# SwiGLU feed-forward on one core: the first rows of x by plain loads and TensorE transposes instead of transposing loads

**Chip, cores, metric.** One core of a Trainium2 chip (trn2). The metric is the device time of one execution in microseconds (us). One core has no neighbour to compare with here, so an execution is called slow only when it lies over 1.5% above the fastest of the same kernel. The kernel before spreads over some 2% by itself (127.79 to 130.0 in 16 executions), so for it the rule cuts the top of an even spread rather than a separate state.

## The reference

```python
B, S, D, F = 1, 2048, 512, 1376          # bf16
def reference(x, w_gate, w_up, w_down):
    g = silu(x @ w_gate)
    u = x @ w_up
    return (g * u) @ w_down
```

## The kernel before

S is cut into 4 blocks of 512 rows, F into 11 tiles of 128 (the last has 96). A unit is one F tile of one block: 4 gate matmuls and 4 up matmuls over the 4 columns of 128 of D (c0 to c3), then silu on ScalarE and the product on VectorE. After 11 units, four row tiles go through the down matmuls. The matmuls need x transposed, which the load does.

```python
N_WARM = 7
xt_pieces = [(0, 0, NDC // 2), (0, NDC // 2, NDC)] + [(cs, 0, NDC) for cs in range(1, NCS)]

def xt_piece(eng, i):                       # transposing load
    cs, c0, c1 = xt_pieces[i]
    eng.dma_start_transpose(
        out=xT_sb[:, cs, c0:c1, :],
        in_=x2d[cs * NT : (cs + 1) * NT, c0 * P : c1 * P],
    ).then_inc(xt_sems[i], 16)

# SyncE's queue
xt_piece(sp, 0)
xt_piece(sp, 1)
for i in range(2, len(w_pieces)):
    w_piece(sp, "g", i)
    w_piece(sp, "u", i)
wd_load(sp)
for i in range(2, len(xt_pieces)):
    xt_piece(sp, i)
# ... cut: the stores of the output

# ScalarE's queue: the first weights
w_piece(act, "g", 0); w_piece(act, "u", 0); w_piece(act, "g", 1); w_piece(act, "u", 1)

# TensorE
def stage1(u):
    cs, fi = divmod(u, NFC)
    pi = piece_of(fi * P)
    wait_w("wg", pi)
    for c in range(NDC):
        wait_xt(cs, c)
        mm1(u, c, "g", (act_done, u - 1) if (c == 0 and u >= 2) else None)
    wait_w("wu", pi)
    for c in range(NDC):
        mm1(u, c, "u", (dve_done, u - 1) if (c == 0 and u >= 2) else None)

for i in range(N_WARM):
    pe.matmul(ps_w[:, 0, :], lhsT=ones_w, rhs=ones_m, start=True, stop=True)
# ... cut: 4 blocks of 11 x stage1 and 4 x stage2
```

## Time and profile before

| | before |
|---|---|
| time, 16 executions | 127.79 to 130.0, median 129.04 |
| the four known at the prediction | 127.96, 127.99, 128.12, 129.66 |
| span of the profiled execution | 126.2 (its time 127.96) |
| TensorE busy | 119.0 (94%) |
| second transposing load of x lands | 8.45 |
| second unit's up half issues, at full speed | 12.12 |

The profiled span is some 1.8 us shorter than the time, which has a fixed part (1.76 us here, 1.77 in the profiled execution after). The prediction shows the lines; L160 in them is line 160 of the kernel, and PEq is TensorE's sequencer. Where the prediction and the expectations speak of a lost window or of one more window, it is a stretch at half speed like the one in this trace, 3.41 us from 8.06 to 11.47. The lines are read in this order: TensorE's row of slices says where TensorE is not full, the chain in order of time says what it waited for there, and the distance between starts of matmuls says how fast the array ran. A row `start us, us, ... x4` merges four instructions: divide by the distance to the next row, not by the length printed, since the records overlap (383 ns each on the page, for matmuls that start 216 ns apart).

### The profile page before, as it was taken

How to read it: one execution, taken by the hardware profiler on the slowest of the kernel's cores; microseconds unless marked ns; L12 is line 12 of the kernel's file. 1: busy time of each engine (PE TensorE's matmuls, PEld its weight loads, DVE VectorE, ACT ScalarE, POOL GpSimd, SP SyncE). 2: the span in 40 equal slices, each digit the busy share in tenths (PEclk: the TensorE clock that was granted, in tenths of full speed). 3: DMA queues.
4: the chain of work that ended last, by engine and by line, in shares of the span. 5: the costliest groups of instructions: out<-in, count | busy, mean ns of one | idle time of the engine just before them, and what ended most of it. 6: DMA issues, size and time to landing. Idle time of an engine off the chain costs nothing.

```text
span 126.2 us, 1355 instructions
## 1 busy us (share of the span) xinstructions
PE 119.0 (94%) x546; PEld 54.6 (43%) x546; DVE 30.6 (24%) x45; ACT 36.9 (29%) x62; POOL 0.2 (0%) x4
## 2 busy tenths in 40 slices
PE   7349999999999999999999999999999999999992
PEld 2013444454444444454444444454444444454471
DVE  0002433342002433342002433442002333442001
ACT  0302233331214333331213333321313333321330
POOL 0000000000000000000000000000000000000000
PEclk9976999999999999999999999999999999999999
DMA  4999999700121000000121000000121000000112
GB/s 79 233 308 370 358 269 242 145 5 0 42 83 42 0 0 0 5 0 0 42 82 42 3 0 0 5 3 0 42 74 51 0 0 0 5 0 0 42 60 64
DMA packets 16438, 8.51 MB, mean 67 GB/s; under 512 B 9808, under 2 KB 16432, under 8 KB 16432
## 3 DMA queue, kind: packets, MB, share of 16 engines
q1 hardware_dynamic: 14320, 7.64, 22.1%
q10 hardware_dynamic: 2112, 0.79, 2.9%
q8 instruction: 4, 0.07, 0.2%
q14 instruction: 2, 0.02, 0.0%
HBM read 4.23 MB, written 2.10 MB: 50 GB/s over the span
## 4 chain that ended last, share of the span: by engine, by line
PE 91%; DMA 5%; SPq 1%; DVE 0%; issue 0%
PE ps_u L160 31%; PE ps_g L160 30%; PE ps_o L194 28%; DMA xT_sb<-in_x_dram 5%; PE ps_w L212 2%; SPq L95 1%; DVE o_sb L286 0%
## 5 line engine op out<-in xcount | busy, mean ns | idle before, releaser
L275 DVE TENSOR_TENSOR hT_sb<-sg_sb,ps_u 128x512 bf16<-128x512 f32 (+1 forms) x44 | 30.2, 687 | 84.7 <-PE ps_u L160 84.7
L160 PE MATMUL ps_g<-xT_sb,wg_sb 128*128 128x512 bf16 (+1 forms) x176 | 46.0, 383 | 4.0 <-DMA xT_sb<-in_x_dram 4.0
L160 PE MATMUL ps_u<-xT_sb,wu_sb 128*128 128x512 bf16 (+1 forms) x176 | 46.1, 385 | 0.0
L248 ACT ACTIVATE sg_sb<-ps_g 128x512 f32<-128x512 f32 (+1 forms) x44 | 26.2, 597 | 52.2 <-PE ps_g L160 52.2
L194 PE MATMUL ps_o<-wd_sb,hT_sb 128*128 128x512 bf16 (+1 forms) x165 | 36.3, 379 | 0.0
L160 PEld LDWEIGHTS ps_g<-xT_sb,wg_sb 128*128 128x128 bf16 (+1 forms) x176 | 17.6, 101 | 25.9 <-issue 3.9
L160 PEld LDWEIGHTS ps_u<-xT_sb,wu_sb 128*128 128x128 bf16 (+1 forms) x176 | 17.8, 101 | 21.0 <-issue 1.1
L194 PEld LDWEIGHTS ps_o<-wd_sb,hT_sb 128*128 128x128 bf16 (+1 forms) x165 | 16.1, 98 | 19.5
L253 ACT CAST o_sb<-ps_o 128x512 bf16<-128x512 f32 x15 | 8.8, 585 | 30.3 <-PE ps_o L194 30.3
L222 PE MATMUL ps_w<-const-bfloat16-1.0 128*128 128x512 bf16 x7 | 3.1, 627 | 0.8 <-PEq L302 0.8
L286 DVE CAST o_sb<-ps_w 128x256 bf16<-128x256 f32 x1 | 0.4, 425 | 8.9 <-PE ps_w L212 8.9
L212 PE MATMUL ps_w<-wd_sb,hT_sb 128*128 128x256 bf16 (+1 forms) x22 | 2.6, 272 | 0.0
L212 PEld LDWEIGHTS ps_w<-wd_sb,hT_sb 128*128 128x128 bf16 (+1 forms) x22 | 2.1, 98 | 0.5
L240 ACT ACT_TABLE_LOAD x1 | 1.3, 1283 | 2.9 <-issue 2.9
L222 PEld LDWEIGHTS ps_w<-const-bfloat16-1.0 128*128 128x128 bf16 x7 | 0.9, 138 | 2.1 <-issue 2.1
L262 ACT CAST o_sb<-ps_w 128x256 bf16<-128x256 f32 x1 | 0.4, 372 | 0.6 <-PE ps_w L212 0.6
L240 ACT ACTIVATE scr<-const-float32-0.0 128x4 f32<-128x4 f32 x1 | 0.2, 205 | 0.0
L302 POOL MEMSET const-bfloat16-1.0<- 128x1 bf16 x1 | 0.1, 101 | 0.0
L302 POOL MEMSET const-uint8-127<- 128x1 uint8 x1 | 0.1, 101 | 0.0
L302 POOL MEMSET const-float32-0.0<- 128x1 f32 x1 | 0.1, 98 | 0.2 <-issue 0.2
L302 POOL MEMSET const-float32-1.0<- 128x1 f32 x1 | 0.1, 98 | 0.0
## 6 DMA issues: line engine op xcount, KB each, us to landing
out_dram<-o_sb SPq DMA_DIRECT2D x15, 128.0 KB, 1.7
wd_sb<-in_w_down_dram SPq DMA_DIRECT2D x1, 1280.0 KB, 11.2
wg_sb<-in_w_gate_dram SPq DMA_DIRECT2D x1, 608.0 KB, 8.0
wu_sb<-in_w_up_dram SPq DMA_DIRECT2D x1, 608.0 KB, 8.3
wg_sb<-in_w_gate_dram SPq DMA_DIRECT2D x1, 384.0 KB, 6.4
wu_sb<-in_w_up_dram SPq DMA_DIRECT2D x1, 384.0 KB, 6.9
wg_sb<-in_w_gate_dram ACTq DMA_DIRECT2D x1, 256.0 KB, 5.0
wu_sb<-in_w_up_dram ACTq DMA_DIRECT2D x1, 256.0 KB, 6.4
```

Of the source, the lines that this page charges most:

```text
L95: eng.dma_start_transpose(out=xT_sb[:, cs, c0:c1, :], in_=x2d[cs * NT : (cs + 1) * NT, c0 * P : c1 * P],).then_inc(xt_sems[i], 16)
L160: ins = pe.matmul(ps[0:fw, b, :], lhsT=w_sb[:, c, f0 : f0 + fw], rhs=xT_sb[:, cs, c, :], start=(c == 0), stop=(c == NDC - 1),)
L194: ins = pe.matmul(ps_o[:, b, 0:D], lhsT=hT_sb[0:fw, fi, bk * P : (bk + 1) * P], rhs=wd_sb[0:fw, fi, :], start=(fi == 0), stop=(fi == NFC - 1),
L212: ins = pe.matmul(ps_w[:, h, 0:HD], lhsT=hT_sb[0:fw, fi, bk * P : (bk + 1) * P], rhs=wd_sb[0:fw, fi, h * HD : (h + 1) * HD], start=(fi == ...
L222: pe.matmul(ps_w[:, 0, :], lhsT=ones_w, rhs=ones_m, start=True, stop=True)
L240: act.activation(out=scr[:, 0:4], in_=zero_c, func=SILU)
L248: ins = act.activation(out=sg_sb[0:fw, b, :], in_=ps_g[0:fw, b, :], func=SILU)
L253: ins = act.copy(out=o_sb[:, bk, :], in_=ps_o[:, bk % 2, 0:D])
L262: ins = act.copy(out=o_sb[:, bk, 0:HD], in_=ps_w[:, 0, 0:HD])
L275: ins = dve.tensor_tensor(out=hT_sb[0:fw, fi, cs * NT : (cs + 1) * NT], in0=sg_sb[0:fw, b, :], in1=ps_u[0:fw, b, :], op=MULT,)
L286: ins = dve.tensor_copy(out=o_sb[:, BL, HD:D], in_=ps_w[:, 1, 0:HD])
L302: nc = _bacc.Bacc("TRN2", target_bir_lowering=False, num_devices=1)
```

## The change

The intent is to start real work earlier: load the first 512 rows as they lie (in the trace of the kernel before, a plain load of 128 KB issued at 0.73 landed 2.7 us later, and the transposing load of 256 KB issued beside it let TensorE start only at 6.05), transpose them on TensorE, which is idle then (for the 2.13 us before 6.05), and use each column of 128 as soon as it is copied back. Row 4p + j of x goes to column j x 128 + p, and the first four output tiles are stored in the same order, so the result is unchanged. The core of the diff:

```diff
+N_WARM2 = 2
+    x0r = x2d[0:NT, :].rearrange("(p j) d -> p j d", j=JB)
+    o0r = o2d[0:NT, :].rearrange("(p j) d -> p j d", j=JB)
-        ps_w = psum("ps_w", [P, 2, 512], F32)
+        ps_tr = psum("ps_tr", [P, 2, 2, JB, P], BF16)
+        def x0_piece(eng, c):
+            eng.dma_start(
+                x0_sb[:, :, c * P : (c + 1) * P], x0r[:, :, c * P : (c + 1) * P]
+            ).then_inc(x0_sems[c], 16)
 # SyncE
-            xt_piece(sp, 0)
-            xt_piece(sp, 1)
-            for i in range(2, len(w_pieces)):
+            x0_piece(sp, 0)
+            w_piece(sp, "g", 0)
+            x0_piece(sp, 2)
+            for i in range(1, len(w_pieces)):
                 w_piece(sp, "g", i)
                 w_piece(sp, "u", i)
 # ... cut: w_down's load, as before
+            sp.wait_ge(wu_sems[-1], 16)
+            sp.wait_ge(wd_sems[0], 16)
 # ... cut: then the transposing loads of blocks 1 to 3, the stores
 # GpSimd: the identity
+            pool.memset(ident[:], 0.0).then_inc(id0_sem, 1)
+            pool.wait_ge(id0_sem, 1)
+            pool.affine_select(out=ident[:], in_=ident[:], ...).then_inc(id_sem, 1)
 # TensorE
+            def tr_group(c):
+                pe.wait_ge(x0_sems[c], 16)
+                for jj in range(JB):
+                    ins = pe.transpose(
+                        out=ps_tr[:, c % 2, 0, jj, :],
+                        in_=x0_sb[:, jj, c * P : (c + 1) * P],
+                        identity=ident[:],
+                    )
+                    if jj == 0 and c >= 2:
+                        ins._wait_ge(tr_evac, c - 1)
+                ins.then_inc(tr_ready, 1)
+            warm(N_WARM)
+            pe.wait_ge(id_sem, 1)
+            tr_group(0)
+            tr_group(1)
+            warm(N_WARM2)
+            wait_w("wg", 0)
+            mm1(0, 0, "g", (tr_evac, 1))
+            wait_w("wu", 0)
+            mm1(0, 0, "u")
+            mm1(0, 1, "g", (tr_evac, 2))
+            mm1(0, 1, "u")
+            tr_group(2)
+            tr_group(3)
+            mm1(0, 2, "g", (tr_evac, 3))
+            mm1(0, 2, "u")
+            mm1(0, 3, "g", (tr_evac, 4))
+            mm1(0, 3, "u")
 # ScalarE's queue
-            w_piece(act, "g", 0)
+            x0_piece(act, 1)
             w_piece(act, "u", 0)
-            w_piece(act, "g", 1)
-            w_piece(act, "u", 1)
+            x0_piece(act, 3)
 # VectorE, before its products
+            def tr_evacuate(c):
+                ins = dve.tensor_copy(
+                    out=xT_sb[:, 0, c, :].rearrange("q (j p) -> q j p", p=P),
+                    in_=ps_tr[:, c % 2, 0, :, :],
+                )
+                ins._wait_ge(tr_ready, c + 1)
+                ins.then_inc(tr_evac, 1)
```

Cut: the last two half blocks use ps_g and ps_u instead of ps_w, which is gone.

More of the change, by code (lines that the diff above doesn't have):

```diff
@@ L60, in sem @@
             return es.enter_context(nc.semaphore(name))
+        x0_sb = sb("x0_sb", [P, JB, D], BF16)
         xT_sb = sb("xT_sb", [P, NCS, NDC, NT], BF16)
@@ L68, in bass_standalone__swiglu_ffn__prompt_kernel @@
         o_sb = sb("o_sb", [P, NB, D], BF16)
+        ident = sb("ident", [P, P], BF16)
         scr = sb("scr", [P, 8], F32)
@@ L77, in bass_standalone__swiglu_ffn__prompt_kernel @@
         zero_c = nc.const_aps.tensor(0.0, [P, 4], F32)
-        xt_pieces = [(0, 0, NDC // 2), (0, NDC // 2, NDC)] + [(cs, 0, NDC) for cs in range(1, NCS)]
-        xt_sems = [sem("xt_sem%d" % i) for i in range(len(xt_pieces))]
+        x0_sems = [sem("x0_sem%d" % i) for i in range(NDC)]
+        xt_sems = [None] + [sem("xt_sem%d" % i) for i in range(1, NCS)]
         wg_sems = [sem("wg_sem%d" % i) for i in range(len(w_pieces))]
@@ L83, in bass_standalone__swiglu_ffn__prompt_kernel @@
         wd_sems = [sem("wd_sem%d" % i) for i in range(2)]
+        id_sem = sem("id_sem")
+        id0_sem = sem("id0_sem")
+        tr_ready = sem("tr_ready")
+        tr_evac = sem("tr_evac")
         g_ready = sem("g_ready")
@@ L91, in bass_standalone__swiglu_ffn__prompt_kernel @@
         out_sem = sem("out_sem")
-        def xt_piece(eng, i):
-            cs, c0, c1 = xt_pieces[i]
-            eng.dma_start_transpose(
-                out=xT_sb[:, cs, c0:c1, :],
-                in_=x2d[cs * NT : (cs + 1) * NT, c0 * P : c1 * P],
-            ).then_inc(xt_sems[i], 16)
+        def x0_piece(eng, c):
+            eng.dma_start(
+                x0_sb[:, :, c * P : (c + 1) * P], x0r[:, :, c * P : (c + 1) * P]
+            ).then_inc(x0_sems[c], 16)
         def w_piece(eng, which, i):
@@ L105, in w_piece, with out_rows @@
                 eng.dma_start(wu_sb[:, :, a:b], wur[:, :, a:b]).then_inc(wu_sems[i], 16)
-        def wd_load(eng):
-            eng.dma_start(wd_sb[:, 0:NFULL, :], wdr).then_inc(wd_sems[0], 16)
-            if NFULL < NFC:
-                eng.dma_start(
-                    wd_sb[0 : fws[-1], NFULL, :], w_down[NFULL * P : F, :]
-                ).then_inc(wd_sems[1], 16)
+        def out_rows(bk):
+            if bk < JB:
+                return o0r[:, bk, :]
+            return o2d[bk * P : (bk + 1) * P, :]
         BL = NB - 1
@@ L117, in _ @@
         def _(sp):
-            xt_piece(sp, 0)
-            xt_piece(sp, 1)
-            for i in range(2, len(w_pieces)):
+            x0_piece(sp, 0)
+            w_piece(sp, "g", 0)
+            x0_piece(sp, 2)
+            for i in range(1, len(w_pieces)):
                 w_piece(sp, "g", i)
                 w_piece(sp, "u", i)
-            wd_load(sp)
-            for i in range(2, len(xt_pieces)):
-                xt_piece(sp, i)
-            sp.wait_ge(xt_sems[-1], 16)
-            for b in range(BL):
-                sp.dma_start(o2d[b * P : (b + 1) * P, :], o_sb[:, b, :]).then_inc(
-                    out_sem, 16
-                )._wait_ge(o_evac, b + 1)
-            sp.dma_start(o2d[BL * P : (BL + 1) * P, 0:HD], o_sb[:, BL, 0:HD]).then_inc(
+            sp.dma_start(wd_sb[:, 0:NFULL, :], wdr).then_inc(wd_sems[0], 16)
+            if NFULL < NFC:
+                sp.dma_start(
+                    wd_sb[0 : fws[-1], NFULL, :], w_down[NFULL * P : F, :]
+                ).then_inc(wd_sems[1], 16)
+            sp.wait_ge(wu_sems[-1], 16)
+            sp.wait_ge(wd_sems[0], 16)
+            if NFULL < NFC:
+                sp.wait_ge(wd_sems[1], 16)
+            for cs in range(1, NCS):
+                sp.dma_start_transpose(
+                    out=xT_sb[:, cs, :, :], in_=x2d[cs * NT : (cs + 1) * NT, :]
+                ).then_inc(xt_sems[cs], 16)
+            sp.wait_ge(xt_sems[NCS - 1], 16)
+            for bk in range(BL):
+                sp.dma_start(out_rows(bk), o_sb[:, bk, :]).then_inc(out_sem, 16)._wait_ge(
+                    o_evac, bk + 1
+                )
+            sp.dma_start(out_rows(BL)[:, 0:HD], o_sb[:, BL, 0:HD]).then_inc(
                 out_sem, 16
             )._wait_ge(o_evac, BL + 1)
-            sp.dma_start(o2d[BL * P : (BL + 1) * P, HD:D], o_sb[:, BL, HD:D]).then_inc(
+            sp.dma_start(out_rows(BL)[:, HD:D], o_sb[:, BL, HD:D]).then_inc(
                 out_sem, 16
@@ L137, in _ @@
             sp.wait_ge(out_sem, 16 * (NB + 1))
+        @block.gpsimd
+        def _(pool):
+            pool.memset(ident[:], 0.0).then_inc(id0_sem, 1)
+            pool.wait_ge(id0_sem, 1)
+            pool.affine_select(
+                out=ident[:],
+                in_=ident[:],
+                compare_op=mybir.AluOpType.not_equal,
+                fill=1.0,
+                base=0,
+                pattern=[[-1, P]],
+                channel_multiplier=1,
+            ).then_inc(id_sem, 1)
         @block.tensor
         def _(pe):
-            state = {"wg": -1, "wu": -1, "wd": False, "xt": -1}
+            state = {"wg": -1, "wu": -1, "wd": False}
+            def tr_group(c):
[9 more added lines that the diff above has]
+                ins.then_inc(tr_ready, 1)
             def wait_w(kind, pi):
@@ L146, in wait_w @@
                     state[kind] = pi
-            def wait_xt(cs, c):
-                for i, (pcs, c0, c1) in enumerate(xt_pieces):
-                    if pcs == cs and c0 <= c < c1 and state["xt"] < i:
-                        pe.wait_ge(xt_sems[i], 16)
-                        state["xt"] = i
             def mm1(u, c, which, first_wait=None):
@@ L175, in stage1 @@
                 pi = piece_of(fi * P)
+                if fi == 0:
+                    pe.wait_ge(xt_sems[cs], 16)
                 wait_w("wg", pi)
                 for c in range(NDC):
-                    wait_xt(cs, c)
                     mm1(u, c, "g", (act_done, u - 1) if (c == 0 and u >= 2) else None)
@@ L209, in stage2_last @@
                 for h in range(2):
+                    ps = (ps_g, ps_u)[h]
                     for fi in range(NFC):
@@ L212, in stage2_last @@
                         ins = pe.matmul(
-                            ps_w[:, h, 0:HD],
+                            ps[:, 0, 0:HD],
                             lhsT=hT_sb[0:fw, fi, bk * P : (bk + 1) * P],
@@ L219, in stage2_last, with warm @@
                     ins.then_inc(o_ready, 1)
-            for i in range(N_WARM):
-                pe.matmul(ps_w[:, 0, :], lhsT=ones_w, rhs=ones_m, start=True, stop=True)
+            def warm(n):
+                for i in range(n):
+                    pe.matmul(ps_o[:, 1, :], lhsT=ones_w, rhs=ones_m, start=True, stop=True)
+            warm(N_WARM)
[15 more added lines that the diff above has]
+            mm1(0, 3, "u")
+            for u in range(1, NFC):
+                stage1(u)
             for cs in range(NCS):
-                for fi in range(NFC):
-                    stage1(cs * NFC + fi)
+                if cs > 0:
+                    for fi in range(NFC):
+                        stage1(cs * NFC + fi)
                 for jj in range(JB):
@@ L261, in _ @@
                     if bk == BL:
-                        ins = act.copy(out=o_sb[:, bk, 0:HD], in_=ps_w[:, 0, 0:HD])
+                        ins = act.copy(out=o_sb[:, bk, 0:HD], in_=ps_g[:, 0, 0:HD])
                         ins._wait_ge(o_ready, bk + 1)
@@ L269, in _ @@
         def _(dve):
+            def tr_evacuate(c):
+                ins = dve.tensor_copy(
+                    out=xT_sb[:, 0, c, :].rearrange("q (j p) -> q j p", p=P),
+                    in_=ps_tr[:, c % 2, 0, :, :],
+                )
+                ins._wait_ge(tr_ready, c + 1)
+                ins.then_inc(tr_evac, 1)
             def mul(u):
@@ L282, in mul @@
                 ins.then_inc(dve_done, 1)
+            for c in range(NDC):
+                tr_evacuate(c)
             for u in range(NU):
                 mul(u)
-            ins = dve.tensor_copy(out=o_sb[:, BL, HD:D], in_=ps_w[:, 1, 0:HD])
+            ins = dve.tensor_copy(out=o_sb[:, BL, HD:D], in_=ps_u[:, 0, 0:HD])
             ins._wait_ge(o_ready, BL + 2)
```

## The prediction

> **What bounds the kernel now.** I read the summary first, to see which engine is the wall and in which slices it is not.
>
> ```profile
> PE 119.0 (94%) x546; PEld 54.6 (43%) x546; DVE 30.6 (24%) x45; ACT 36.9 (29%) x62; POOL 0.2 (0%) x4
> PE   7349999999999999999999999999999999999992
> PEclk9976999999999999999999999999999999999999
> ```
>
> A slice is 126.2 / 40 = 3.155 us. TensorE is full from the fourth slice to the last, so nothing but TensorE matters there. The holes are in slices 1 to 3, and the granted clock is low in slices 3 and 4. Next I read the chain of waits in order of time (start us, length us, what), to see what fills the opening:
>
> ```profile
> 0.73 1.31 SPq L95
> 2.09 6.36 DMA xT_sb<-in_x_dram
> 8.50 1.03 PE ps_g L160 x2
> 9.53 1.71 PE ps_u L160 x4
> 12.28 0.86 PE ps_u L160 x4
> ...
> 123.79 0.42 DVE o_sb L286
> ```
>
> The second transposing load of x (128 x 2 x 512) lands at 8.45 and starts the chain of matmuls. After that, four matmuls take 0.86 us (0.216 each) without a gap to the end, but the four at 9.53 take 1.71, exactly twice that. The timeline and the table of windows (length, busy of the engines, PEclk, DMA share, GB/s) say why:
>
> ```profile
> 0.77 3.15 PE L222 MATMUL ps_w<-const-bfloat16-1.0 128*128 128x512 bf16 x7 [0.77 <-PEq L302]
> 6.05 0.59 PE L160 MATMUL ps_g<-xT_sb,wg_sb 128*128 128x512 bf16 x2 [2.13 <-DMA xT_sb<-in_x_dram]
> 8.50 1.03 PE L160 MATMUL ps_g<-xT_sb,wg_sb 128*128 128x512 bf16 x2 [1.85 <-DMA xT_sb<-in_x_dram]
> 12.12 1.03 PE L160 MATMUL ps_u<-xT_sb,wu_sb 128*128 128x512 bf16 x4
> ```
>
> ```profile
> 8.00:8.10 0.10, 0.00 (x0) 0.00 (x0) 0.00 (x0) 0.00 (x0) 0.00 (x0) 0.81 1.11 264
> 8.10:8.20 0.10, 0.00 (x0) 0.00 (x0) 0.00 (x0) 0.00 (x0) 0.00 (x0) 0.50 0.98 300
> 11.40:11.50 0.10, 0.10 (x2) 0.04 (x1) 0.10 (x1) 0.00 (x0) 0.00 (x0) 0.62 0.93 316
> 11.50:11.60 0.10, 0.10 (x2) 0.07 (x1) 0.10 (x1) 0.00 (x0) 0.00 (x0) 1.00 1.16 402
> ```
>
> The warm-up matmuls end near 3.9; TensorE then does two matmuls in 4.6 us, and the clock is halved from about 8.06 to 11.47, 3.41 us, just when the work arrives. So the opening costs twice: a wait for the load, then half speed. My reference point is 12.12: there the up half of the second unit issues at full speed, and from it to the end the two kernels do the same work.
>
> [...]
>
> **The change part by part.** It removes the two transposing loads of the first 512 rows from the path. These rows now come by four plain loads of 128 KB, are transposed by 16 TensorE transposes against an identity that GpSimd makes, and are copied out of PSUM by four VectorE copies. It reorders the first unit so that gate and up matmuls run as each copy is done, adds two warm-ups, and holds the other three transposing loads until all weights have landed. The end is the same but for the PSUM tiles of the last half blocks.
>
> *Loads.* The new pieces have the shape of the first weight pieces (128x4x128), which the trace times from issue to landing, beside the bandwidth of the opening:
>
> ```profile
> wg_sb<-in_w_gate_dram ACTq DMA_DIRECT2D x1, 128.0 KB, 2.7
> wu_sb<-in_w_up_dram ACTq DMA_DIRECT2D x1, 128.0 KB, 3.8
> xT_sb<-in_x_dram SPq DMA_TRANSPOSE x5, 5.2
> 4.50:5.00 0.50, 0.00 (x0) 0.00 (x0) 0.00 (x0) 0.00 (x0) 0.00 (x0) 1.00 1.10 249
> ```
>
> A transposing load of 256 KB took 5.2 us; a plain one of 128 KB issued at the same 0.73 took 2.7, beside it. So the first pieces of x, one on each queue, land at 0.73 + 2.7 = 3.4. Summing the windows, 0.85 MB had moved by 5.5 in the kernel before; x's four pieces with the first gate and up pieces are 0.79 MB. My estimates: first weights at 4.4, the second pair of x pieces at 5.5. The later weights are ahead of their use: the second gate piece is 0.26 MB more, some 1 us at 249 GB/s, so about 6.5.
>
> *VectorE copies.* What is known is this (mean ns of one):
>
> ```profile
> L286 DVE CAST o_sb<-ps_w 128x256 bf16<-128x256 f32 x1 | 0.4, 425 | 8.9 <-PE ps_w L212 8.9
> L275 DVE TENSOR_TENSOR hT_sb<-sg_sb,ps_u 128x512 bf16<-128x512 f32 x40 | 27.5, 687 | 80.6 <-PE ps_u L160 80.6
> ```
>
> 262 ns for 256 more elements is about one a ns, over a fixed 0.16 us. The new copy takes 512 bf16 elements: 0.43 us at two a ns [...], 0.69 at one. I take 0.43 as the more likely.
>
> *The opening, step by step* (estimates, us). Warm-ups issue from 0.77 to 0.77 + 7 x 0.427 = 3.76; x is there at 3.4. The identity is two GpSimd instructions of 128 elements a partition; started near 0.7 they have 3 us, so I take them as hidden. Four transposes at the low clock, paced by their weight loads (0.15 each at this clock in the timeline, for the warm-ups), are 0.5: the first group is through at 4.3, its copy runs 4.4 to 4.85. The second group ends at 4.75, its copy runs 4.9 to 5.35. [...]the two extra warm-ups take 0.43, to 5.2. Then gate c0 and up c0 to 5.6; gate c1, free since 5.4, and up c1 to 6.05. The pieces for groups 3 and 4 came at 5.5. At 0.08 to 0.1 a transpose, these groups end at 6.4 and 6.75; their copies run 6.55 to 7.0 and 7.05 to 7.5. Gate c2 starts at 7.1, gate c3 at 7.55, and up c3 ends at 8.0. The second unit then issues its gate half from 8.0 and its up half at 8.0 + 0.86 = 8.86. The reference point moves from 12.12 to 8.86: **3.26 us gained**. Four of the matmuls that ran at half speed run at full speed in it, and the removed wait is the rest, less the new chain of transposes and copies.
>
> *Beside other work, so nothing.* The later transposing loads: weights land near 17.5 instead of 18.5, and the three loads, last landed at 24.9 in the kernel before, were issued from 12.1 to 22.3. With about 2 us of issue each from 17.5 and 5 to landing, the first comes near 23 and the last near 28. The first is needed when the second stage-1 block starts, 38.0 - 3.3 = 34.7. The output's row order changes, not its transfers' size. The PSUM tiles of the last half blocks change, not their counts.
>
> So the sum is 128.05 - 3.26 = 124.8, if all goes well.
>
> **The rivals.**
> 1. *The copies run at one element a ns.* Each is 0.26 longer, and they are in the path: gate c1 waits for the second, gate c3 for the fourth. The same chain gives gate c1 at 5.9, gate c3 near 8.35 and the up half near 9.65: 2.5 gained, 125.6. For it: VectorE ran near one a ns in both rows above. Against: those are fp32. I give it a third.
> 2. *The clock falls in the new opening.* [...] If it falls, 3.41 us at half speed come from the full stretch after 8, costing 1.7: about 126.5. I give it an eighth. One of the four times before is 129.66, just 1.65 over the others, which could be one such window more; it speaks for a phase that moves between executions.
> 3. *The loads come later.* Packets of x are 256 bytes, and six loads compete. At 150 GB/s the third pair lands near 7.3, groups 3 and 4 start there and the up half is near 10.1: 2.0 gained, 126.0. Against: the windows from 2.4 to 3.0, with packets of the same size, show 233 to 246 GB/s. A fifth, mostly milder. A late identity would have the same effect, but would have to be over 3 us.
> 4. *The load was hidden anyway*, with no gain. The chain of waits is against it: all of TensorE's work follows the landing without another wait. Three in a hundred.
>
> **Range and chances.** The good case is 124.8 and the slow copies 125.6; weighted two to one that is 125.05, and the tails of rivals 2 and 3 are above, so I predict 125.1. The low end, 124.5, is the chain with copies and transposes all a little quicker; the high end, 126.7, is one lost window. Faster by over 2% asks for less than 0.98 x 128.05 = 125.49. The good case has 0.7 us to spare and the slow-copy case just misses, as do a lost window and badly late loads: 0.65 for faster, 0.33 within, 0.02 slower.
>
> **What would show each step.** Right: the first transposes start at 3.8 and the third group near 6; the up half of the second unit issues at 8.9 (8.6 to 9.7); the copies last near 0.43; PEclk is low nowhere after 4.7; every four matmuls take 0.86 from there to the end; the chain's share of transposing loads is 0. Rival 1 shows as copies of 0.69 with TensorE waiting for VectorE; rival 2 as PEclk of 0.5 for 3.4 us after 8; rival 3 as TensorE waiting for loads of x or weights between 4 and 8. I would be wrong altogether if the later transposing loads, now held back, were late for the second block: TensorE would wait near 35 for a load.

## The result

125.21 us median of 11 executions (124.65 to 125.6), against 129.04 of 16 (127.79 to 130.0) of the kernel before. The ratio is 0.9725, 95% interval 0.9686 to 0.9764: faster. A ratio is one of means of fast executions (here 125.19 over 128.72, the mean of the thirteen of the sixteen that are called fast), so it is not quite the ratio of the medians. The predicted 125.1 stands. Two things deserve notice: the kernel before turned out to be about 1 us slower in the middle than its profiled execution, and to spread over 2.2 us where the new kernel spreads over 1.

The summary of the changed kernel:

```profile
PE 119.5 (97%) x564; PEld 55.4 (45%) x564; DVE 32.2 (26%) x49; ACT 36.9 (30%) x62; POOL 0.7 (1%) x6
PE   7979999999999999999999999999999999999992
PEclk9999999999999999999999999999999999999999
```

TensorE's row is now full from slice 4 on; the first slice, with the start, and the third are thin, and no low clock is recorded. The chain in order of time for the first 14 us (start us, us, what) ends its opening here:

```profile
2.18 4.88 DMA x_sb<-in_x_dram
...
7.20 0.40 PE ps_tr L176 x4
...
7.62 0.44 DVE xT_sb L330
...
8.11 0.39 PE ps_g L196
8.50 0.22 PE ps_u L196
8.71 0.86 PE ps_g L196 x4
9.58 0.86 PE ps_u L196 x4
```

The chain runs through the last of the four plain loads: it is issued at 2.18 and lands at 7.06. Then come the fourth group of transposes (0.40 us for the four), its copy, and the matmuls on c3. The timeline shows TensorE itself (start us, us, what, in brackets what it sat idle for):

```profile
3.97 0.85 PE L176 MATMUL ps_tr<-ident,x_sb 128*128 128x128 bf16 x8
5.09 0.38 PE L196 MATMUL ps_g<-xT_sb,wg_sb 128*128 128x512 bf16 x1
6.37 0.38 PE L176 MATMUL ps_tr<-ident,x_sb 128*128 128x128 bf16 x4 [0.21 <-DMA x_sb<-in_x_dram]
7.20 0.38 PE L176 MATMUL ps_tr<-ident,x_sb 128*128 128x128 bf16 x4 [0.45 <-DMA x_sb<-in_x_dram]
9.41 1.03 PE L196 MATMUL ps_u<-xT_sb,wu_sb 128*128 128x512 bf16 x4
```

The reference point moved from 12.12 to 9.41, 2.71 us, and the span from 126.2 to 123.5, 2.7 us: the whole difference of the two traces lies before that point. The groups give the copy:

```profile
L330 DVE COPY xT_sb<-ps_tr 128x512 bf16<-128x512 bf16 x4 | 1.6, 421 | 6.4 <-PE ps_tr L176 6.4
```

### The profile page after: what moved, and what is told of

Read it like the earlier page. It is cut to its first block, busy times and chain, and to the rows that moved or that the text cites. A ratio compares the mean times of both kernels' runs of the same rounds, so it can differ in the third digit from the quotient of the medians.

```text
span 123.5 us, 1406 instructions
## 1 busy us (share of the span) xinstructions
PE 119.5 (97%) x564; PEld 55.4 (45%) x564; DVE 32.2 (26%) x49; ACT 36.9 (30%) x62; POOL 0.7 (1%) x6
## 4 chain that ended last, share of the span: by engine, by line
PE 92%; DMA 4%; ACTq 1%; DVE 1%; issue 0%
PE ps_g L196 30%; PE ps_u L196 30%; PE ps_o L231 29%; DMA x_sb<-in_x_dram 4%; PE ps_u L250 1%; PE ps_g L250 1%; ACTq L112 1%; ACTq L103 1%; DVE xT_sb L330 0%; DVE o_sb L355 0%; PE ps_tr L176 0%
## 5 line engine op out<-in xcount | busy, mean ns | idle before, releaser
L261 PE MATMUL ps_o<-const-bfloat16-1.0 128*128 128x512 bf16 x9 | 3.7, 572 | 0.8 <-PEq L371 0.8
L330 DVE COPY xT_sb<-ps_tr 128x512 bf16<-128x512 bf16 x4 | 1.6, 421 | 6.4 <-PE ps_tr L176 6.4
L176 PE MATMUL ps_tr<-ident,x_sb 128*128 128x128 bf16 x16 | 1.6, 246 | 0.7 <-DMA x_sb<-in_x_dram 0.7
L176 PEld LDWEIGHTS ps_tr<-ident,x_sb 128*128 128x128 bf16 x16 | 1.2, 113 | 2.2 <-issue 2.2
L261 PEld LDWEIGHTS ps_o<-const-bfloat16-1.0 128*128 128x128 bf16 x9 | 1.1, 129 | 2.1 <-issue 2.1
L250 PE MATMUL ps_g<-wd_sb,hT_sb 128*128 128x256 bf16 (+1 forms) x11 | 1.4, 272 | 0.0
L250 PE MATMUL ps_u<-wd_sb,hT_sb 128*128 128x256 bf16 (+1 forms) x11 | 1.4, 273 | 0.0
L250 PEld LDWEIGHTS ps_g<-wd_sb,hT_sb 128*128 128x128 bf16 (+1 forms) x11 | 1.1, 98 | 0.3
L250 PEld LDWEIGHTS ps_u<-wd_sb,hT_sb 128*128 128x128 bf16 (+1 forms) x11 | 1.1, 98 | 0.1
```

The lines of the kernel that those rows point to most:

```text
L176: ins = pe.transpose(out=ps_tr[:, c % 2, 0, jj, :], in_=x0_sb[:, jj, c * P : (c + 1) * P], identity=ident[:],)
L250: ins = pe.matmul(ps[:, 0, 0:HD], lhsT=hT_sb[0:fw, fi, bk * P : (bk + 1) * P], rhs=wd_sb[0:fw, fi, h * HD : (h + 1) * HD], start=(fi == 0) ...
L261: pe.matmul(ps_o[:, 1, :], lhsT=ones_w, rhs=ones_m, start=True, stop=True)
L330: ins = dve.tensor_copy(out=xT_sb[:, 0, c, :].rearrange("q (j p) -> q j p", p=P), in_=ps_tr[:, c % 2, 0, :, :],)
```

## The experiments

Twelve runs were made, on four chips; all gave the reference's result. Times are medians of 6 executions unless told otherwise. The changed kernel itself gave 125.21, and 125.36 on another chip, so differences of a few tenths between calls mean little, and times of the kernel before move with its spread (its means in the calls are 128.9 to 129.5).

### Parting the gain: the clock alone, the order alone, both

**The clock held.** The kernel before, with more warm-ups:

```diff
-N_WARM = 7
+N_WARM = 13
+N_FILL = 6
                 for c in range(NDC):
+                    if u == 0 and c == NDC // 2:
+                        for i in range(N_FILL):
+                            pe.matmul(ps_w[:, 1, :], lhsT=ones_w, rhs=ones_m, start=True, stop=True)
                     wait_xt(cs, c)
```

> The kernel before, with 13 warm-up matmuls instead of 7 and 6 more of them while TensorE waits for the second load of x; nothing else. It parts the two halves of the gain: the load still lands near 8.45 us, only the clock is held. Theory (wait plus clock): the clock stays at 1.00 from 4.7 us on, the up half of the second unit issues at about 10.6 instead of 12.12 (8.5 + 6 x 0.216 + 4 x 0.216), the span falls from 126.2 by 1.5 us to 124.7, and the slow half of the executions of the kernel before (near 129.6, where others take 128.1) is gone, if that half is a clock that fell at another moment. Rival (the clock does not matter, only the landing of x does): the same time as before, 128 to 129.7, still in two groups. Rival (the phase can't be held by warm-ups): PEclk of 0.5 somewhere in 5 to 12 us.

127.03 (126.72 to 127.35), ratio 0.9847 (0.9805 to 0.9888). The timeline of TensorE:

```profile
0.77 5.08 PE L226 MATMUL ps_w<-const-bfloat16-1.0 128*128 128x512 bf16 x13 [0.77 <-PEq L306]
8.71 0.60 PE L161 MATMUL ps_g<-xT_sb,wg_sb 128*128 128x512 bf16 x2 [0.90 <-DMA xT_sb<-in_x_dram]
10.88 1.03 PE L161 MATMUL ps_u<-xT_sb,wu_sb 128*128 128x512 bf16 x4
```

The load lands even a little later (the matmuls start at 8.71 instead of 8.50), and still the up half of the second unit issues at 10.88 instead of 12.12: from 9.15 on, four matmuls follow four every 0.86 us. The time fell by 2.0 us against the mean (129.0), more than the 1.5 expected, which was drawn from the trace of a fast execution (127.96); and the spread went too: 0.6 us in six executions instead of 2.3 in 27. So about half of the whole gain is the clock (in the two traces it is 12.12 - 10.88 = 1.24, with a landing 0.21 later). Of the expectation one part was wrong: the kernel before is not in two groups (27 executions fill 128.14 to 130.4 without a clear gap). The record has a hint of what varies, the mean recorded clock of each of them: it is 0.973 in six, which took 129.2 to 129.93, and 1.00 in the rest. The prediction's execution, with 3.41 of 126.2 us at half speed, has 0.986, so 0.973 is by my estimate from these two figures twice that time.

**The order alone.** The kernel before with gate c and up c interleaved in the first unit:

```diff
+            wait_w("wg", 0)
+            for c in range(NDC):
+                wait_xt(0, c)
+                mm1(0, c, "g")
+                wait_w("wu", 0)
+                mm1(0, c, "u")
 # ... cut: the loop over units then leaves out the first
```

> The kernel before with only the order of the first unit changed as the change does it: gate c, up c for each of the four columns, so that two up matmuls run at 6 us in the wait for the second load. Theory: two matmuls fewer after the landing, at the low clock 2 x 0.427 = 0.85 us earlier; [...] Expected 0.85 us off (127.2) if it falls, 1.9 us off (126.2) if not. Rival (order is worth nothing): 0.

128.68 of 22 executions (127.93 to 130.06), ratio 0.9982 (0.9959 to 1.0005): the same, a miss. The profiled execution happens to be one in which the clock never rose in the opening:

```profile
6.16 0.59 PE L160 MATMUL ps_g<-xT_sb,wg_sb 128*128 128x512 bf16 x1 [2.25 <-DMA xT_sb<-in_x_dram]
6.54 0.63 PE L160 MATMUL ps_u<-xT_sb,wu_sb 128*128 128x512 bf16 x1
...
10.89 1.87 PE L160 MATMUL ps_g<-xT_sb,wg_sb 128*128 128x512 bf16 x4
12.60 1.03 PE L160 MATMUL ps_u<-xT_sb,wu_sb 128*128 128x512 bf16 x4
13.46 1.03 PE L160 MATMUL ps_g<-xT_sb,wg_sb 128*128 128x512 bf16 x4
```

The four gate matmuls from 10.89 to 12.60 take 1.71, half speed, and the next four 0.86. In the kernel before the same seven warm-ups at the same 0.77 had raised the clock by 6.05 (two matmuls in 0.59, a start every 0.2). Up to there the two programs are the same, so the moment at which the clock rises differs between the two executions. That this spreads the times of the kernel before is borne out by the run with the clock held (0.6 us against 2.3). My expectation had an error, too: the low clock ended at 11.47 in the kernel before, after about seven matmuls of the two units at half speed, and near 12.6 here, after twelve. By my estimate from these two it ends at a moment and not after a number of matmuls, and then two matmuls taken out before that moment save 2 x 0.216 = 0.43, not 2 x 0.427. Savings of 0 to 0.53 us lie inside the interval, so this run doesn't show that the order is worth nothing. The load in this execution landed at 9.16, 0.7 later than in the trace of the kernel before. The page's clock row and the table of windows read 1.00 throughout this opening; only the distance between starts shows the low clock. The same holds for the warm-ups of the kernel before: seven in 3.15 us, 0.43 apart, with 1.00 in the table from 0.00 to 3.41.

**Both.** Warm-ups and order together, still with the transposing loads:

```diff
-N_WARM = 7
+N_WARM = 13
+N_FILL = 5
             for c in range(NDC):
+                if c == NDC // 2:
+                    for i in range(N_FILL):
+                        pe.matmul(ps_w[:, 1, :], lhsT=ones_w, rhs=ones_m, start=True, stop=True)
                 wait_xt(0, c)
                 mm1(0, c, "g")
```

> The kernel before with both of the cheap parts: 13 warm-ups and 5 more in the wait (the clock held), and the first unit's gate and up matmuls interleaved. What it leaves out is the plain loads with transposes, so the distance from here to the changed kernel (125.2) is what those are worth alone. Theory (with the clock held, two matmuls fewer after the landing are worth 2 x 0.216 = 0.43): 126.6, against 127.0 with the clock held alone; left for the plain loads 1.4 us. Rival (the order is worth nothing without the early x, as the run with the order alone seemed to say with 0.2): 127.0.

126.26 (125.96 to 127.06), ratio 0.9758 (0.9707 to 0.9809). This ratio is the exception: the fastest execution of the kernel before was 127.58, so that six of its eleven are called slow, and 0.9758 agrees with the mean of all eleven (129.49); over the five fast ones (128.73) it would be 0.982. With the clock held the order is worth 127.03 - 126.26 = 0.77, somewhat more than the 0.43 expected, but the landing of x moved (8.71 and 8.45), which is 0.26 of it: between the traces the up half of the second unit moves from 10.88 to 10.18, 0.70, and 0.44 is left for the order. What the plain loads are worth beyond these two cheap edits is 126.26 - 125.21 = 1.05 by the medians, 0.7 by the spans (124.2 and 123.5), and about 0.4 by the ratios (0.9758 and 0.9725 of 129), or 1.2 with 0.982: between 0.4 and 1.2 us, and no better known than that. No run keeps all else and exchanges only the kind of load.

### The same parts, taken out of the changed kernel

**The old order.** Gate c0 to c3 as the copies are done, then up c0 to c3:

```diff
             mm1(0, 0, "g", (tr_evac, 1))
-            wait_w("wu", 0)
-            mm1(0, 0, "u")
             mm1(0, 1, "g", (tr_evac, 2))
-            mm1(0, 1, "u")
             tr_group(2)
             tr_group(3)
             mm1(0, 2, "g", (tr_evac, 3))
-            mm1(0, 2, "u")
             mm1(0, 3, "g", (tr_evac, 4))
-            mm1(0, 3, "u")
+            wait_w("wu", 0)
+            for c in range(NDC):
+                mm1(0, c, "u")
```

> The changed kernel with the first unit in the old order: gate c0 to c3 as the copies are done, then up c0 to c3. Theory: three up matmuls that ran in waits now run after gate c3, so the end moves by 3 x 0.216 = 0.65 us later (124.1 span against 123.5). Rival (order is worth nothing, because the wait for the x pieces sets all): under 0.2 us.

126.04 (125.67 to 126.05), span 124.2 against 123.5. 0.7 to 0.8 us lost, as expected: in the changed kernel three up matmuls run in waits for loads and copies.

**No warm-ups.**

```diff
-N_WARM = 7
-N_WARM2 = 2
+N_WARM = 0
+N_WARM2 = 0
```

> The changed kernel without any warm-up matmuls (0 and 0). The early x is kept, the clock is not. Theory: the opening runs at the low clock [...]: transposes and matmuls in the chain are about twice as long, 0.7 to 1.0 us later in all (126.1 without counting the fixed part: 125.2 + 0.9). Rival [...]: one more window at half speed, 2.4 us later, 127.6. Rival (waits for loads hide the low clock): under 0.3 us.

126.78 (126.01 to 126.95): 1.5 later, between the theory's 0.9 and the rival's 2.4. The first transposes start at 4.23; the timeline then has the matmuls of the first unit at half speed, 0.43 apart:

```profile
5.73 0.63 PE L196 MATMUL ps_u<-xT_sb,wu_sb 128*128 128x512 bf16 x1
6.16 0.63 PE L196 MATMUL ps_g<-xT_sb,wg_sb 128*128 128x512 bf16 x1
...
10.91 1.03 PE L196 MATMUL ps_u<-xT_sb,wu_sb 128*128 128x512 bf16 x4
```

The clock rises near 10.3 here, as the four gate matmuls from 9.85 to 10.91 take 1.06 instead of 0.86. The transposes run at the clock of the moment as well: eight in a row took 1.01 us here, and 0.61 in the repeat of the changed kernel. What makes the clock rise when it does is not shown by this run.

### The term that was off: when x lands

**Two pieces of x.** The pieces are 256 KB with rows of 512 bytes, one at the head of each queue, ahead of the weights:

```diff
-                x0_sb[:, :, c * P : (c + 1) * P], x0r[:, :, c * P : (c + 1) * P]
+                x0_sb[:, :, c * HD : (c + 1) * HD], x0r[:, :, c * HD : (c + 1) * HD]
 # ... cut: each two groups of transposes wait for one piece
             x0_piece(sp, 0)
             w_piece(sp, "g", 0)
-            x0_piece(sp, 2)
             x0_piece(act, 1)
             w_piece(act, "u", 0)
-            x0_piece(act, 3)
```

> The changed kernel with x's first 512 rows loaded in two pieces of 256 KB (512-byte rows), one at the head of each queue, instead of four of 128 KB with weight pieces between; TensorE's order is kept. Theory (my step that failed is the landing of the second pair of x pieces, taken as 5.5 and measured at 6.3 and 7.1): all x is there before the third group is due at 6.0, the up half of the second unit issues at 8.7 instead of 9.4, 0.7 us faster than the changed kernel. Rival (the copies or TensorE's own chain set it, not the loads): under 0.2 us. Rival (the first transposes start later, as each first piece is twice as long): a part of it is given back, 0.2 to 0.5 us faster.

126.88: five executions at 126.72 to 127.1, one at 125.27. Slower, against every theory. The timeline shows why:

```profile
5.00 1.01 PE L175 MATMUL ps_tr<-ident,x_sb 128*128 128x128 bf16 x8 [1.08 <-DMA x_sb<-in_x_dram]
6.65 0.63 PE L195 MATMUL ps_g<-xT_sb,wg_sb 128*128 128x512 bf16 x1
7.08 0.63 PE L195 MATMUL ps_u<-xT_sb,wu_sb 128*128 128x512 bf16 x1
```

The first piece, twice as large, lands near 4.9, TensorE pauses for 1.08 us after the warm-ups, and the matmuls from 6.65 to 8.36 are 0.43 apart: the clock has not risen. From 9.52 on they are 0.22 apart. This is the prediction's rival 2 in another form.

**Transposes moved up**, otherwise the same.

```diff
             mm1(0, 0, "u")
+            tr_group(2)
             mm1(0, 1, "g", (tr_evac, 2))
             mm1(0, 1, "u")
-            tr_group(2)
             tr_group(3)
             mm1(0, 2, "g", (tr_evac, 3))
```

> As the run with two pieces, and with the third and fourth group of transposes moved up, one before gate c1 and one before gate c2, so that VectorE copies without a gap. Theory: four copies of 0.42 from 4.7 end at 6.4, up c3 at 7.0, and the second unit's gate half waits for its weight piece, near 7.2; its up half issues near 8.1: 1.3 us faster than the changed kernel. Rival (the weights' landing is the next bound): the gain over the run with two pieces is under 0.3 us and TensorE waits for a weight load.

126.03: three executions at 125.08 to 125.17, three at 126.89 to 127.17. The profiled one is of the fast kind, with a span of 123.3, and no wait for the second unit's weights. Its second unit's up half issues at 9.27, not at the expected 8.1: TensorE waited 0.48 us for x and 0.35 for the first gate weights, so even this kind is only 0.2 to 0.3 us ahead of the changed kernel.

**The same with 10 warm-ups.**

```diff
-N_WARM = 7
+N_WARM = 10
```

> The run with two pieces and moved transposes, with 10 warm-up matmuls instead of 7, so that TensorE does not pause until x lands (between 4.2 and 4.9 us). It tests why the two-piece runs fell into two groups, 125.1 and 127. Theory (x of 256 KB a piece lands up to 1 us later, [...]in about half of the executions the clock is not raised until after 9 us): the slow group is gone, all near 125.0 to 125.4. Rival (the loads themselves come in two speeds): two groups again, 1.8 us apart.

125.21 (124.95 to 125.4), all six together. The slow group is gone with three more warm-ups as the only edit, so it was the clock and not the loads (this call was on another chip than the one before). TensorE now starts later and waits for no load:

```profile
5.08 0.70 PE L175 MATMUL ps_tr<-ident,x_sb 128*128 128x128 bf16 x8
9.39 1.03 PE L195 MATMUL ps_u<-xT_sb,wu_sb 128*128 128x512 bf16 x4
```

**x on one queue, the first weights on the other**, with 9 warm-ups:

```diff
-N_WARM = 10
+N_WARM = 9
 # SyncE's queue
             x0_piece(sp, 0)
-            w_piece(sp, "g", 0)
+            x0_piece(sp, 1)
 # ScalarE's queue
-            x0_piece(act, 1)
+            w_piece(act, "g", 0)
             w_piece(act, "u", 0)
```

> As that, with both x pieces on SP's queue and the first gate and up weights alone on ACT's, and 9 warm-ups: what the first matmul needs (the first half of x, the first gate weights) is then at the head of both queues. Theory (loads set the opening, in the order in which their bytes come): first transposes at 4.2, first gate matmul near 5.2, the up half of the second unit at 8.4 instead of 9.4: 1.0 us faster than the changed kernel, 124.3. Rival (the second unit's weights become the bound): 0.3 to 0.6 us faster, with a wait for a gate or up weight load at 7 to 8.

125.01 (124.62 to 125.38), ratio 0.9693 (0.9646 to 0.974): the fastest, 0.2 to 0.35 us ahead of the changed kernel, within what differs between calls, and not the 1.0 expected. The timeline:

```profile
4.56 0.79 PE L175 MATMUL ps_tr<-ident,x_sb 128*128 128x128 bf16 x8
9.00 1.03 PE L195 MATMUL ps_u<-xT_sb,wu_sb 128*128 128x512 bf16 x4
```

No wait for a load is left. From the first transpose to the reference point it takes 9.00 - 4.56 = 4.44, against 9.41 - 3.97 = 5.44 in the changed kernel: 1.0 less, but the start is 0.6 later, because TensorE was still in its nine warm-ups until 4.56. The stretch doesn't tell what the queues are worth: with x on both queues and ten warm-ups it was 9.39 - 5.08 = 4.31, shorter still, since with a later start the loads have landed. What remains is TensorE's own work and the copies.

### Three controls

**The changed kernel once more**, unedited.

> The changed kernel as it is, for comparison on this chip: 125.2 us, spread under 1 us, no execution 1.7 us above the others (which would be a lost window of the clock).

125.36 (125.07 to 125.47), ratio 0.9711 (0.9683 to 0.9739): as it was. But its trace waits for other loads than the first trace did, the first piece of x and the first gate weights, and not for the last piece of x:

```profile
4.29 0.82 PE L176 MATMUL ps_tr<-ident,x_sb 128*128 128x128 bf16 x8 [0.36 <-DMA x_sb<-in_x_dram]
6.07 0.38 PE L196 MATMUL ps_g<-xT_sb,wg_sb 128*128 128x512 bf16 x1 [0.53 <-DMA wg_sb<-in_w_gate_dram]
```

Its second unit's up half issues at 9.62. So which load of the opening comes last changes from one execution to the next.

**Each copy done twice**, the first into a spare buffer, as a copy at half speed would be:

```diff
 # ... cut: the spare buffer x2_sb
+                first = dve.tensor_copy(
+                    out=x2_sb[:, c, :].rearrange("q (j p) -> q j p", p=P),
+                    in_=ps_tr[:, c % 2, 0, :, :],
+                )
+                first._wait_ge(tr_ready, c + 1)
                 ins = dve.tensor_copy(
```

> The changed kernel with each of the four copies done twice, the first time to a spare buffer (as a copy at half speed would be; the result stays right). Prediction's rival 1, and its claim that the second and fourth copies are in the path: 0.8 us later if both are, 0.45 if only the fourth is (the doubled second copy ends before the third x piece lands at 6.3), 0 if the loads hide them all.

125.78 (125.7 to 125.9) against 125.36: 0.42 later, the size of the "only the fourth copy" case. The trace doesn't put it there, though: TensorE waits 0.63 us for the third pair of copies, before gate c2 (0.30 in the repeat's trace). A pair takes 0.75 (its second copy overlaps the first at its ends) and costs less than the 0.8 that the prediction's rival 1 gave for copies of 0.69. That part of it hides in waits for loads is likely, but not shown.

**Without the hold** of the three later transposing loads:

```diff
-            sp.wait_ge(wu_sems[-1], 16)
-            sp.wait_ge(wd_sems[0], 16)
-            if NFULL < NFC:
-                sp.wait_ge(wd_sems[1], 16)
```

> The changed kernel without the hold: the three later transposing loads are issued right behind the weights, as the kernel before did. The prediction counts the hold as costing and gaining nothing, as these loads are due at 34 and land by 28. Expected: the same time within 0.2 us; the loads land some 2 us earlier. Rival (transposing loads beside weights slow the weights that TensorE waits for): slower, with a wait of TensorE for a weight load between 12 and 20 us.

125.28 (125.11 to 125.69), no wait of TensorE for a weight. The last of these loads lands at 25.0 instead of 26.8. The hold costs and gains nothing.

## Why the prediction was right, step by step

- **The wait on the transposing load is on the path, and goes.** Right: its share of the chain is gone, and all of the gain in span (2.7) lies before 9.41.
- **The opening costs twice, wait and clock.** Right, and the larger surprise is how much is clock: holding it alone gives 2.0 of the 3.8 us between the medians. The prediction's working has it too small: it speaks of four matmuls at half speed, but the ten from 8.50 to 12.12 took 3.62 us in its trace, against 2.16 at 0.216 each, so about seven ran at half speed, worth 1.46. Its sum of 3.26 isn't touched by this, as it is a difference of two moments. It also left out that the moment at which the clock rises moves: it was up by 6.05 in its trace, and not before 12.6 in the run with the order alone. Its remark on the one time of 129.66 was the right hint.
- **Copies at two elements a ns, 0.43.** Right: 421 ns for 512 bf16 elements (L330), where the trace before had 425 ns for 256 of fp32 (L286). The rate was an assumption when it was made, as that trace had no copy of bf16. Rival 1 falls.
- **Beside other work, so nothing.** Right: the held transposing loads land by 26.8, TensorE has no wait near 35, and without the hold the time is the same.
- **The clock stays up in the new opening (rival 2).** Right in every execution of the changed kernel, none of which lies 1.7 us above the others; in the trace the two extra warm-ups at 4.66 already start 0.22 apart. That it would rise so early was my estimate, which the trace before does not show: there it is up by 6.05. And the two-piece runs are slow in five of six executions and then in three of six. The slow one that was profiled pauses for 1.08 us before the first transposes; with pauses of 0.36 and 0.48, in the repeat of the changed kernel and in the run with the transposes moved up, the matmuls after it are at full speed. The eighth that I gave it was not too much.
- **The second pair of x pieces lands at 5.5.** Wrong: this is the mis-sized term that reached the reference point in the profiled execution. The first pair was late, too (3.8 and 4.2 instead of 3.4), but the warm-ups covered most of it there: the transposes start at 3.97 instead of 3.8. The issues, with the median time to landing:

```profile
x_sb<-in_x_dram SPq DMA_DIRECT2D x2, 128.0 KB, 3.6
x_sb<-in_x_dram ACTq DMA_DIRECT2D x2, 128.0 KB, 4.2
wg_sb<-in_w_gate_dram SPq DMA_DIRECT2D x1, 256.0 KB, 4.7
```

And from the table of windows, the first 5.5 us (length, busy of the engines, PEclk, DMA share, GB/s):

```profile
0.00:5.50 5.50, 4.67 (x19) 1.97 (x20) 0.75 (x2) 1.49 (x2) 0.70 (x6) 1.00 0.67 143
```

143 GB/s over 5.5 us is 0.79 MB, just the sum that I took for x and the first weights. The bandwidth was right. What I left out is that the second weight pieces, issued on SyncE's queue at 2.69 and 3.36, were already moving beside the third load of ScalarE's queue. That one lands at 7.06, when 1.25 MB have moved (the next windows show 274 GB/s to 6.30 and 320 to 7.06). So the third group starts at 6.37 instead of about 6.05, the fourth at 7.20 instead of 6.4, the fourth copy at 7.62 instead of 7.05, and the reference point is at 9.41 instead of 8.86. These 0.55 us are the whole difference between the chain's 3.26 and the measured 2.71. It is rival 3 in its mild form. That weights overtook x is inferred from bytes and landings of one trace, not seen packet by packet, and no run isolates it: the run with x on one queue has no wait for x, but neither has the run with ten warm-ups and x on both. In the repeat of the same kernel it was the first gate weights that came late (5.93 instead of 4.4). What holds in both traces is that the opening's loads land later than the prediction had them.
- **The sum.** 124.8 + 0.55 = 125.35, and the profiled execution took 125.27. The prediction of 125.1 had 0.3 us on top of 124.8, most of it for slow copies, which did not come; late loads took their place with 0.55. The path was foreseen, but that the figure fits to 0.1 us is luck. The gain against the kernel before is larger than predicted (ratio 0.9725, predicted 125.1 / 128.05 = 0.977) because 128.05, a median of four, was a low draw of a kernel that spreads over 2.2 us.

## What to carry to other kernels

A short opening can lose twice, by the wait and by the clock that is low after it (2.13 and 1.85 us of wait here, then 3.41 at half speed); price them apart, and first try the edit that costs nothing, more filler matmuls up to the landing (2.0 of 3.8 us here) and an order that uses the wait (0.4 to 0.8 once the clock was held, nothing clear without). When several loads feed the first work, count the bytes of everything that is issued on both queues before the last piece that you need, not only the bytes that you need (1.25 MB had moved here when the last piece of x landed; I had counted 0.79). And when a kernel's times spread more than its profile explains, look for a clock state that differs between executions (a mean clock of 0.973 in six of 27 here) before trusting a median of four.
